# Sign words on GpSimd, a table of shifts for the jobs of two layers, and dummy transposes at the start

## The chip, the cores and the metric

The kernel runs on one core of a Trainium2 chip. The metric is device time in microseconds (us) from start to end of one execution of the whole program. A run of three executions gives a median; beside it stands one further execution that was profiled, and its trace is what this text reads. Engines are called by the names of the profile: PE is the matrix engine (PEld its weight loads), DVE the vector engine, ACT the scalar engine, POOL is GpSimd, SP issues DMAs.

## The reference

Three layers run one after the other on 2304 tokens of width 512 (4 sequences of 576 tokens).

```python
# attention, 8 heads of 64, with rotary positions on q and k
scores = scale * q_rot @ k_rot.T;  attn = softmax(scores);  x = attn @ v
# gated layer, d_ff 1536
gate = 1.0 / (1.0 + np.exp(-(x @ w_gate)))
x = (gate * (x @ w_val)) @ w_out
# third layer, d_ff 1024
h = x @ w_in
solu = h * softmax(h)
y = layernorm(solu) * g_ln @ w_out
```

Activations and results are float32. The five weight matrices arrive as float64.

## The kernel before

**Stages.** Attention runs from 0 to about 290 us over 16 pairs of heads; the gated layer follows to about 716 us and the third layer to the end. Products are made from float32 operands split in a high and a low part (each operand is cast once, and the cast is subtracted from the operand for the low part), so that three matmuls stand for one product; the gated layer and the third layer further use sums of blocks so that seven block products do the work of eight. That leaves much element-wise work for DVE, ACT and POOL: `xst` (sums of blocks of x, L535), `xs` (its cast on ACT, L540, and the subtraction on DVE, L544), `held` (copies of PSUM that a later matmul group needs, L1363), `yst` (copies of finished PSUM banks), `gs` (gate times value).

**Decoding of weights.** A float64 block of 128 x 512 is loaded (`w_load`, an SP DMA) and turned into float32 by integer operations on its two 32-bit words, in `decode`. `w_mag` on ACT (L463) makes the magnitude of the high word; `w_sign` on DVE (L466) takes the sign bit of the high word into the destination; `w_or_mag` (L469) and `w_or_low` (L474), both on DVE, then put magnitude and low word into it. Destinations are the buffers that the trace calls `w` and `rawv`. From `w`, DVE, ACT and POOL make sums (L483) and splits (cast in `w_high`, L486; subtraction in `w_low`, L494, on DVE or POOL). 52 blocks pass through this; 6 of them during attention, in a separate place of the code.

**What sets the order.** Every operation is written down as a job with engine, cost, buffers read and written, and a due time `need`. For the later two layers `run_jobs` (quoted below) places the jobs one by one: PE's jobs stay in the order written; on each other engine, of the jobs ready at the earliest time, the one with the smallest due time goes first; jobs that name two engines go where they can start first. Each engine's instructions then stand in the program in that order, and an engine runs them in that order: an instruction that waits holds up all behind it. POOL also issues the DMAs `yd<-yst` of the gated layer (L1457). Attention has an order of its own, from a table that this change does not touch, so that a job's cost there decides nothing about the order.

**The start.** PE begins with transposes of the first rows of q and k (`tq`, L222, by the matrix `ident`), then the scores `s` (L291), while DVE and ACT copy the transposes out (`st`), reduce (L298) and exponentiate (L303).

## Time and profile before

| | us |
|---|---|
| median of three executions | 914.72 (914.27 to 915.67) |
| the profiled execution | 915.11 |
| its span, first to last instruction | 913.2 |
| PE busy in it | 882.9 (97%) |
| DVE busy | 810.2 (89%) |
| ACT busy | 653.5 (72%) |
| POOL busy | 339.3 (37%) |

The profiled execution took 915.11 us, 0.39 us above the median; 1.9 us of it lie around the span, before the first instruction and after the last one. The shares are means over three stages that differ much, so the text below reads them by stretch.

### The profile page before, as it was taken

Reading aid. Unit: us, or ns where it says so; the run is one execution under the profiler, and the core shown is the slowest. Engines: PE = TensorE matmul, PEld = TensorE weight load, DVE = VectorE, ACT = ScalarE, POOL = GpSimd, SP = SyncE. Lnnn points to the kernel's source line nnn. Section 1 sums busy time; section 2 is a strip of 40 time slices with the busy share of each in tenths; the row PEclk is TensorE's granted clock in tenths of the full one; section 3 lists DMA queues with packets and bytes.
Section 4 is the critical chain, followed back from the end, with each engine's and each line's share of the span. In section 5 each row is a group of like instructions: output and inputs, shape, how many; then the busy total and the mean of one; then the engine's idle time right before and its main releaser. Section 6 shows DMA issues by size and latency. Waiting matters only on the chain.

```text
span 913.2 us, 16106 instructions
## 1 busy us (share of the span) xinstructions
PE 882.9 (97%) x5354; PEld 833.1 (91%) x5354; DVE 810.2 (89%) x1523; ACT 653.5 (72%) x1379; POOL 339.3 (37%) x296
## 2 busy tenths in 40 slices
PE   4999999999999999999999999999999999999998
PEld 3999999999998999999999999999999877888886
DVE  5999999999997798999998999999987499999971
ACT  4999999999995465666667666666565276777751
POOL 7679899898845000011011121212030243233200
PEclk9999999999999999999999999999999999999999
DMA  4667777678663762425275864659599834454332
GB/s 127 159 183 196 205 200 197 184 209 214 155 165 112 221 216 81 151 81 196 86 230 135 260 133 145 129 174 229 179 250 364 185 124 93 99 109 81 81 70 46
DMA packets 120882, 147.33 MB, mean 161 GB/s; under 512 B 44752, under 2 KB 90080, under 8 KB 120800
## 3 DMA queue, kind: packets, MB, share of 16 engines
q1 hardware_dynamic: 113888, 136.87, 51.4%
q0 software_dynamic: 6912, 9.44, 7.1%
q8 instruction: 42, 0.69, 0.3%
q14 instruction: 40, 0.33, 0.1%
HBM read 77.76 MB, written 37.30 MB: 126 GB/s over the span
## 4 chain that ended last, share of the span: by engine, by line
PE 73%; DVE 19%; issue 3%; DMA 2%; ACT 2%; POOL 0%; SPq 0%; DVEq 0%; ACTq 0%
PE s L291 9%; PE av L420 8%; PE te L379 7%; DVE xs L544 2%; PE tq L222 2%; PE far_c L1869 2%; PE far_b L1869 2%; PE far_c L1871 2%; PE far_b L1870 2%; PE far_c L1870 2%; PE far_b L1871 2%; PE tk L400 1%; DVE w L469 1%; PE near_a L630 1%; PE near_a L629 1%
## 5 line engine op out<-in xcount | busy, mean ns | idle before, releaser
L298 DVE TENSOR_REDUCE nm<-s 128x1 f32<-128x576 f32 x144 | 108.2, 752 | 11.5 <-PE s L291 9.0
L303 ACT ACTIVATE e<-s,nm 128x576 f32<-128x576 f32 x144 | 107.7, 748 | 7.4 <-DVE nm L298 6.0
L291 PE MATMUL s<-st 128*128 128x288 f32 x512 | 96.6, 312 | 5.5 <-DVE st L251 3.9
L373 DVE TENSOR_TENSOR et<-te,et 128x512 fp32r<-128x512 f32 x144 | 95.8, 676 | 1.4 <-ACT et L370 1.3
L420 PE MATMUL av<-et,vs 128*128 128x288 f32 x512 | 94.4, 312 | 0.4 <-POOL vs L202 0.4
L1457 POOL DMA_DIRECT2D yd<-yst x40 | 36.0, 1280 | 141.1 <-ACT yst L486 141.1
L370 ACT CAST et<-te 128x512 fp32r<-128x512 f32 x144 | 81.2, 587 | 7.8 <-PE te L379 6.4
L379 PE MATMUL te<-ident,e 128*128 128x128 f32 x576 | 81.9, 274 | 2.5 <-DVE et L373 2.4
L291 PEld LDWEIGHTS s<-st 128*128 128x128 f32 x512 | 75.1, 193 | 6.8 <-ACT st L249 4.2
L420 PEld LDWEIGHTS av<-et,vs 128*128 128x128 f32 x512 | 73.3, 191 | 0.7 <-POOL vs L202 0.6
L379 PEld LDWEIGHTS te<-ident,e 128*128 128x128 f32 x576 | 67.4, 141 | 5.1 <-DVE et L373 2.5
L540 ACT CAST xs<-xst 128x384 fp32r<-128x384 f32 x110 | 50.7, 518 | 13.7 <-DVE xst L535 11.5
L544 DVE TENSOR_TENSOR xs<-xst,xs 128x384 fp32r<-128x384 f32 x112 | 56.4, 548 | 2.2 <-ACT xs L540 2.0
L1538 POOL TENSOR_TENSOR xs<-xst,xs 128x512 fp32r<-128x512 f32 (+1 forms) x14 | 17.5, 1254 | 72.7 <-ACT xs L1535 72.7
L431 POOL TENSOR_TENSOR x_sb<-uw,um 64x576 f32<-64x576 f32 x30 | 43.2, 1439 | 2.5 <-DMA um<-uw 0.4
L494 POOL TENSOR_TENSOR wv<-w,wv 128x512 fp32r<-128x512 f32 (+1 forms) x3 | 5.2, 1743 | 103.3 <-ACT wv L486 103.3
L170 POOL TENSOR_TENSOR turned_t<-raw_t,other_t 128x576 f32<-128x576 f32 (+1 forms) x30 | 40.5, 1369 | 1.2
L463 ACT ACTIVATE mag<-raw_w 128x512 f32<-128x512 f32 x52 | 34.9, 676 | 7.9 <-DMA raw_w<-in_moe_w_val_dram 3.7
L162 POOL TENSOR_TENSOR other_t<-raw_t,rope_sb 128x1152 f32<-128x1152 f32 x14 | 37.4, 2674 | 5.6 <-DMA raw_t<-in_q_dram 4.5
L162 POOL TENSOR_TENSOR raw_t<-raw_t,rope_sb 128x1152 f32<-128x1152 f32 x14 | 37.3, 2664 | 1.1
L1811 POOL TENSOR_TENSOR st<-st,mhalf 128x1 f32<-128x1 f32 x18 | 15.9, 884 | 54.9 <-DVE st L1810 53.7
L629 PE MATMUL near_a<-xs,wg 128*128 128x384 f32 x96 | 32.3, 337 | 2.1 <-ACT held L1363 2.1
(475 smaller groups left out, 3068.4 us busy)
## 6 DMA issues: line engine op xcount, KB each, us to landing
st<-st SPq DMA_DIRECT2D x45, 288.0 KB, 4.0
xst<-xd SPq DMA_DIRECT2D x32, 384.0 KB, 6.0
raw_w<-in_moe_w_out_dram SPq DMA_DIRECT2D x20, 512.0 KB, 4.5
yd<-yst POOLq DMA_DIRECT2D x40, 192.0 KB, 6.5
st<-st SPq DMA_DIRECT2D x47, 144.0 KB, 2.4
raw_w<-in_moe_w_gate_dram SPq DMA_DIRECT2D x12, 512.0 KB, 4.3
raw_w<-in_moe_w_val_dram SPq DMA_DIRECT2D x12, 512.0 KB, 3.7
cd<-mag SPq DMA_DIRECT2D x22, 256.0 KB, 5.5
```

The costliest lines, as they stand in the source:

```text
L162: eng.tensor_mul(out=(o, x)[step], in0=x, in1=w.to_broadcast([P, n, 2, D // 2]))
L291: nc.tensor.matmul(ps[:, j, :HALF], w, x, start=m == 0, stop=m == len(mm) - 1)
L298: nc.vector.tensor_reduce(out=nm, in_=ps[:, :, :HALF], axis=AX.XY, op=ALU.max, negate=True)
L303: nc.scalar.activation(out=e.rearrange("p (j c) -> p j c", j=2), in_=ps[:, :, :HALF], func=AF.Exp, bias=nm, accum_out=sums[i][:, n:n + 1],)
L370: nc.scalar.copy(out=h_out, in_=ps)
L373: nc.vector.tensor_sub(out=l_out, in0=ps, in1=h_out.bitcast(F32))
L379: nc.tensor.transpose(ps[:, r * P:(r + 1) * P], e[:, r * P:(r + 1) * P], ident)
L420: nc.tensor.matmul(av[:, :HALF], *mm[m], start=m == 0, stop=m == len(mm) - 1)
L431: eng.tensor_add(out=x_sb[hp][rows, b * S:(b + 1) * S], in0=uws.pop((i, h))[rows], in1=uws[i][rows])
L540: nc.scalar.copy(out=t[:, 0], in_=here)
L544: l_eng.tensor_sub(out=t[:, 1], in0=here, in1=t[:, 0].bitcast(F32))
L629: nc.tensor.matmul(out, wh, t[:, 0], start=fresh and j == 0, stop=False, skip_group_check=not fresh)
```

## The change

There are four parts. First, `decode` writes a new job `w_zero` on POOL in place of `w_sign` on DVE: the high word, read as a float, times 0.0, which leaves a zero with the word's sign. The job's due time is the same; its cost in the planner is 0.9 and it is not marked as one that holds the port that DVE and POOL share. This concerns 46 of 52 blocks; the 6 in attention stay on DVE. Second, every job of the later two layers gets a name (`place`, and a running number), and a table `SHIFT` of 945 numbers (mean size 8.2 us) is added to the due times by that name. Two offsets `KEEP_I` are smaller. Third, 54 transposes of `ident` into a PSUM bank that nobody reads: 30 before the first `tq`, 10 after the first three, 5, 5 and 4 behind the scores 1, 2 and 3 of the first pair. Fourth, costs and start times of some attention jobs are edited, and one assignment in `qk_bank` is written shorter; neither moves an instruction.

```diff
+    def w_zero(raw, dst):
+        nc.gpsimd.tensor_scalar(out=dst.bitcast(F32), in0=words(raw)[1].bitcast(F32), scalar1=0.0, scalar2=None, op0=ALU.mult)
...
+        idle_ps = ps_av.tile([P, 512], F32, tag="av", name="idle")
+
+        def keep_clock(n):
+            for _ in range(n):
+                nc.tensor.transpose(idle_ps[:, 0:P], ident, ident)
+
+        keep_clock(30)
         first.extend(qk_bank(0, part)[0][2] for part in range(3))
-        pass
+        keep_clock(10)
...
+    IDLE_AFTER = {1: 5, 2: 5, 3: 4}
...
+        def run():
+            found["s", g] = scores(i, n)
+            if i == 0 and n in IDLE_AFTER:
+                keep_clock(IDLE_AFTER[n])
...
+    plain_job, names_of = job, []
+
+    SHIFT = {
+        "again.0.1": -5.9, "again.0.2": -33.5, "again.0.3": -4.4, "again.0.4": -16.7, "again.0.5": -1.4, "again.0.6": -5.6,
...
+    def job(eng, took, fn, reads=(), writes=(), need=0.0, port=None):
+        key = f"{step[0]}.{step[2]}"
+        step[2] += 1
+        names_of.append(key)
+        plain_job(eng, took, fn, reads, writes, need + SHIFT.get(key, 0.0), port)
...
-        job(V, 0.34, lambda: w_sign(raw, dst), (r,), (dst_at,), need - 5, True)
+        job(G, 0.9, lambda: w_zero(raw, dst), (r,), (dst_at,), need - 5, False)
...
-    KEEP_I = {(2, 0): (0, 36.0), (2, 1): (1, 25.0)}
+    KEEP_I = {(2, 0): (0, 30.0), (2, 1): (1, 20.0)}
```

PE's instructions keep their order; only the dummy transposes come in. Its program began like this before, at the very start:

```order
L222 MATMUL tq_0_221<-ident,turned_t 128x128 x4
L222 MATMUL tq_1_226<-ident,turned_t 128x128 x4
L225 MATMUL tq_2_231<-ident,turned_t 128x128
L291 MATMUL s_0_254<-st_0_137 128x288 x4
L291 MATMUL s_1_264<-st_0_137 128x288 x4
L291 MATMUL s_2_279<-st_0_137 128x288 x4
```

And so it begins now:

```order
L674 MATMUL idle<-ident 128x128 x30
L220 MATMUL tq_0_252<-ident,turned_t 128x128 x4
L220 MATMUL tq_1_257<-ident,turned_t 128x128 x4
L223 MATMUL tq_2_262<-ident,turned_t 128x128
L674 MATMUL idle<-ident 128x128 x10
L289 MATMUL s_0_295<-st_0_137 128x288 x4
L289 MATMUL s_1_305<-st_0_137 128x288 x4
L674 MATMUL idle<-ident 128x128 x5
L289 MATMUL s_2_325<-st_0_137 128x288 x4
L674 MATMUL idle<-ident 128x128 x5
```

The dummies need only `ident`; what they stand ahead of is unchanged (line numbers move because the file is longer).

On ACT, at the eleventh group of `held` copies of the gated layer (the profile has it at 575 to 580 us), these rows stood before:

```order
L540 CAST xs_4248<-xst 128x384 x3
L463 ACTIVATE mag_66<-raw_w_65 128x512
L486 COPY yst<-far_a 128x384
L486 COPY yst<-far_b 128x384
L1363 COPY held_4739<-near_a 128x384
L486 COPY yst<-far_d 128x384
L1363 COPY held_4740<-near_c 128x384
```

Now the same place on ACT reads:

```order
L461 ACTIVATE mag_66<-raw_w_65 128x512
L541 CAST xs_4784<-xst 128x384
L541 CAST xs_4303<-xst 128x384 x2
L541 CAST xs_4571<-xst 128x384
L487 COPY yst<-far_b 128x384
L487 COPY yst<-far_a 128x384
L487 COPY yst<-far_d 128x384
L1561 COPY held_4794<-near_a 128x384
L541 CAST xs_4303<-xst 128x384
L487 COPY yst<-far_c 128x384
```

The magnitude went ahead of the casts, and `held<-near_a` now stands behind three copies of `yst`, not two. On DVE, some 10 us earlier in the gated layer, a stretch with two decodes read like this before:

```order
L483 TENSOR_TENSOR w_67<-w_67 128x256 x3
L466 TENSOR_SCALAR w_67<-raw_w_65 128x512
L494 TENSOR_TENSOR wg_4716<-w_67,wg_4716 128x512
L469 SCALAR_TENSOR_TENSOR w_67<-mag_66,w_67 128x512
L494 TENSOR_TENSOR wg_4716<-w_67,wg_4716 128x768
L466 TENSOR_SCALAR w_67<-raw_w_4717 128x512
L544 TENSOR_TENSOR xs_4068<-xst,xs_4068 128x384
L474 SCALAR_TENSOR_TENSOR w_67<-raw_w_65,w_67 128x512
```

The same stretch on DVE now:

```order
L484 TENSOR_TENSOR w_67<-w_67 128x256 x3
L1584 TENSOR_TENSOR gs_1_4792<-far_a,gs_1_4792 128x384
L495 TENSOR_TENSOR wg_4771<-w_67,wg_4771 128x512
L470 SCALAR_TENSOR_TENSOR w_67<-mag_66,w_67 128x512
L495 TENSOR_TENSOR wg_4771<-w_67,wg_4771 128x768
L475 SCALAR_TENSOR_TENSOR w_67<-raw_w_65,w_67 128x512
L545 TENSOR_TENSOR xs_4123<-xst,xs_4123 128x384
L470 SCALAR_TENSOR_TENSOR w_67<-mag_4773,w_67 128x512
```

The two sign words are gone from DVE; the first one now has to be written by POOL between the last sum (L484), which still reads the old `w`, and the `w_or_mag` two rows on (L470). On POOL such a place, with the DMA issues that stand between, reads now:

```order
L467 TENSOR_SCALAR rawv_91<-raw_w_4772 128x512
L1656 DMA yd_147<-yst 128x384 x4
L467 TENSOR_SCALAR w_67<-raw_w_4772 128x512
L467 TENSOR_SCALAR w_67<-raw_w_65 128x512
L1656 DMA yd_147<-yst 128x384 x4
L467 TENSOR_SCALAR w_67<-raw_w_65 128x512
```

Before, POOL had no decode rows there, and the eight DMA issues of one buffer stood together. On ACT, where the third layer starts (the profile has it at 729 to 744 us), the rows before were:

```order
L486 COPY mag_4718<-far_c 128x512
L486 COPY rawv_90<-far_a 128x512
L1535 CAST xs_4068<-xst 128x256
L1535 CAST xs_4068<-xst 128x2x256
L1800 ACT_TABLE_LOAD
L1800 ACTIVATE scr_8760,st_8699<-yst,st_8699 128x1024
L1800 ACTIVATE scr_8761,st_8717<-yst,st_8717 128x1024
```

Now they are:

```order
L487 COPY mag_4773<-far_c 128x512
L2011 ACT_TABLE_LOAD
L2011 ACTIVATE scr_8787,st_8752<-yst,st_8752 128x1024
L2011 ACTIVATE scr_8788,st_8772<-yst,st_8772 128x1024
L1737 CAST xs_4123<-xst 128x256
L487 COPY rawv_90<-far_a 128x512
L2019 ACTIVATE scr_8787,st_8752<-yst,st_8752 128x1024
```

The copy `rawv<-far_a`, which frees a PSUM bank, moved behind the table load and two exponentials. Further on, the copy `mag<-near_c` moved from behind the third exponential to ahead of it. Over the two layers, eight of POOL's `xst` sums (L1544) and its three `wo` subtractions (L1326) moved to DVE, and two 256-wide `xs` subtractions (L1538) the other way.

## Rows read from the trace of the kernel before

**Rows 1.** The page: the span, and the engines' busy time (share, instructions).

```profile
span 913.2 us, 16106 instructions
PE 882.9 (97%) x5354; PEld 833.1 (91%) x5354; DVE 810.2 (89%) x1523; ACT 653.5 (72%) x1379; POOL 339.3 (37%) x296
```

**Rows 2.** Windows: stretch, length, busy time of five engines, granted clock, DMA share, GB/s.

```profile
34.00:280.00 246.00, 245.26 (x1938) 235.72 (x1937) 234.56 (x406) 232.21 (x556) 206.92 (x162) 1.00 0.71 187
340.00:540.00 200.00, 199.41 (x1149) 198.76 (x1148) 185.60 (x371) 135.56 (x291) 21.08 (x20) 1.00 0.51 152
540.00:580.00 40.00, 37.25 (x211) 36.17 (x210) 39.26 (x76) 24.97 (x54) 7.56 (x9) 1.00 0.47 125
```

**Rows 3.** Waits of PE over the whole span: in total, times, longest.

```profile
PE s L291 <- DVE st L251: 3.9, 1, 3.9
...
PE near_a L629 <- ACT held L1363: 2.1, 2, 2.0
PE far_d L1851 <- DVE xs L1860: 1.5, 1, 1.5
PE near_c L1574 <- ACT mag L486: 1.1, 1, 1.1
```

**Rows 4.** Timeline of the start, POOL and PE: start, us, what, idle before.

```profile
1.00 0.29 POOL masks.py:199 TENSOR_SCALAR_AFFINE_SELECT ident<-ident 128x128 f32<-128x128 f32 x1
...
6.89 1.09 PE L222 MATMUL tq<-ident,turned_t 128*128 128x128 f32 x4 [6.89 <-DVE turned_t L170]
...
9.90 0.44 PE L225 MATMUL tq<-ident,turned_t 128*128 128x128 f32 x1
...
31.11 0.60 PE L222 MATMUL tq<-ident,turned_t 128*128 128x128 f32 x4
```

**Rows 5.** Windows of the same kind: six us of the first scores, and the stretch after 580 us.

```profile
18.40:24.80 6.40, 6.31 (x30) 6.28 (x31) 3.22 (x6) 4.15 (x11) 6.32 (x5) 1.00 0.23 51
...
580.40:583.80 3.40, 3.40 (x12) 3.40 (x12) 3.26 (x7) 1.61 (x4) 1.74 (x2) 0.50 1.10 151
```

**Rows 6.** Timeline at 566 us, DVE: a sign word and what follows.

```profile
565.72 0.43 DVE L466 TENSOR_SCALAR w<-raw_w 128x512 int32<-128x512 int32 x1
...
566.06 0.69 DVE L494 TENSOR_TENSOR wg<-w,wg 128x512 fp32r<-128x512 f32 x1
...
566.66 0.68 DVE L469 SCALAR_TENSOR_TENSOR w<-mag,w 128x512 int32<-128x512 int32 x1
```

**Rows 7.** Timeline at 557 us: POOL and DVE side by side.

```profile
557.03 1.28 POOL L494 TENSOR_TENSOR wg<-w,wg 128x512 fp32r<-128x512 f32 x1 [13.68 <-ACT wg L486]
...
557.14 1.72 DVE L469 SCALAR_TENSOR_TENSOR w<-mag,w 128x512 int32<-128x512 int32 x1
```

**Rows 8.** Groups of POOL by shape: busy us, mean ns, idle before.

```profile
L1457 POOL DMA_DIRECT2D yd<-yst x40 | 36.0, 1280 | 141.1 <-ACT yst L486 141.1
...
L494 POOL TENSOR_TENSOR wg<-w,wg 128x256 fp32r<-128x256 f32 x1 | 0.7, 743 | 31.6 <-ACT wg L486 31.6
```

**Rows 9.** Timeline at 575 to 580 us: DVE, ACT and PE.

```profile
575.87 1.45 ACT L540 CAST xs<-xst 128x384 fp32r<-128x384 f32 x3 [1.54 <-DVE xst L535]
...
578.15 0.48 ACT L486 COPY yst<-far_b 128x384 f32<-128x384 f32 x1
578.52 0.49 ACT L1363 COPY held<-near_a 128x384 f32<-128x384 f32 x1
...
579.06 0.44 PE L629 MATMUL near_a<-xs,wg 128*128 128x384 f32 x1 [1.96 <-ACT held L1363]
```

**Rows 10.** Timeline at 729 to 743 us: ACT and PE.

```profile
729.65 0.59 ACT L486 COPY mag<-far_c 128x512 f32<-128x512 f32 x1 [0.96 <-PE far_c L1576]
...
733.49 0.39 PE L1574 MATMUL far_a<-wv,xs 128*128 128x512 f32 x1
...
734.54 1.28 ACT L1800 ACT_TABLE_LOAD   x1
735.83 1.15 ACT L1800 ACTIVATE scr<-yst,st 128x1024 f32<-128x1024 f32 x1
```

More of the change, by code (lines that the diff above doesn't have):

```diff
@@ L214, in qk_bank @@
         raw = turned[i].rearrange("p i h d -> p i (h d)")
-        if part == 0:
-            stacks[i, 0] = st_t[i % 2][0]
-            stacks[i, 1] = st_t[i % 2][1]
+        stacks[i, 0], stacks[i, 1] = st_t[i % 2]
         st = stacks[i, 0]
@@ L730, in job_scores @@
             reads.append(one(f"qtl{i % 2}", 0, 2))
-        took = (1.06 if order[n] is None else 0.53) * (2.0 if g < 4 else 1.0)
+        took = 1.06 if order[n] is None else 0.53
+        if i == 0 and n in IDLE_AFTER:
+            took += 0.11 * IDLE_AFTER[n]
         writes = [one(f"S{g % 2}")] + ([one(f"sum{i % 4}", 0, NTL)] if n == 0 else [])
-        ajob(nc.tensor, took, lambda: found.__setitem__(("s", g), scores(i, n)), reads, writes)
+        def run():
+            found["s", g] = scores(i, n)
+            if i == 0 and n in IDLE_AFTER:
+                keep_clock(IDLE_AFTER[n])
+        ajob(nc.tensor, took, run, reads, writes)
     def job_softmax(g):
@@ L773, in job_attend @@
             e = (A, V)[SLOTS["uw"][2 * h + j]]
-            ajob(e, 0.365 if e is V else 0.3, lambda: high(e, *found["av"][0][1:]), (one("AV"),), (one(uw, *c),))
+            ajob(e, 0.365 if e is V else 0.39, lambda: high(e, *found["av"][0][1:]), (one("AV"),), (one(uw, *c),))
     def job_join(i, h):
@@ L796, in job_weigh_out @@
     def job_weigh_out(i):
-        ajob(V, 0.2, lambda: weigh_out(i, 0), (found.pop(("tr", i)),), (one("rt"),))
+        ajob(V, 0.27, lambda: weigh_out(i, 0), (found.pop(("tr", i)),), (one("rt"),))
         ajob(SP, 0.2, lambda: weigh_out(i, 1), (one("rt"),), (one(f"d{i % 2}"),))
@@ L959 @@
     begin("turned", None)
-    for m, t in enumerate((7.9, 10.0, 10.25)):
+    for m, t in enumerate((7.5, 9.7, 9.85)):
         gate[len(jobs)] = t
@@ L1179, with place @@
     jobs, seen, gate = [], {}, {}
+    plain_job, names_of = job, []
+    SHIFT = {
[156 rows of a table added]
+    }
+    def place(*name):
+        step[:] = [".".join(map(str, name)), None, 0]
+    def job(eng, took, fn, reads=(), writes=(), need=0.0, port=None):
[3 more added lines that the diff above has]
+        plain_job(eng, took, fn, reads, writes, need + SHIFT.get(key, 0.0), port)
     def xs_at(name, j):
@@ L1230, in make_pair @@
     def make_pair(s, n, need):
+        place("pair", s, n)
         for j in range(2):
@@ L1238, in make_plain @@
     def make_plain(n, need):
+        place("plain", n)
         of, done = 1024 * (n % 2), (2, 2, 2, 0)[n]
@@ L1250, in make_again @@
     def make_again(n, need):
+        place("again", n)
         job(SP, 1.7, lambda: nc.sync.dma_start(out=w32[:, 0:1024], in_=wd[n]), (one(f"wd{n}"),), (one("w32", 0, 1024),), need - 12)
@@ L1265, in keep_p @@
     def keep_p(n, need):
+        place("keep", n)
         k = raws_used[0] % 2
@@ L1278, in keep_i @@
     def keep_i(c, need):
+        place("keep_i", c)
         quarter = {f"B{m + 1}{n + 1}": slice(1024 * m + 512 * n, 1024 * m + 512 * n + 512) for m in range(2) for n in range(2)}
@@ L1304, in load_unit @@
     def load_unit(c, need):
+        place("cd", c)
         at_ = C_AT[c]
@@ L1315 @@
     KEEP = {(1, 1): range(0, 5), (1, 2): range(5, 8)}
-    KEEP_I = {(2, 0): (0, 36.0), (2, 1): (1, 25.0)}
+    KEEP_I = {(2, 0): (0, 30.0), (2, 1): (1, 20.0)}
     def make_unit(kind, n, where, need):
+        place("w", kind, n)
         k = raws_used[0] % 2
@@ L1328, in load_x @@
     def load_x(b, need):
+        place("x", *now, b)
         for kk in range(KD):
@@ L1352, in unit @@
     def unit(s, b, n_unit, done=0):
+        place("unit", s, b, n_unit)
         q, kind, setn = n_unit // 2, "gv"[n_unit % 2], n_unit % 2
@@ L1425, in output @@
     def output(s, b, half, setn):
+        place("out", s, b, half)
         bank, need = banks[setn], out_at(s, b, half)
@@ L1463 @@
     END = unit_at(*LAST, 4) + 2 * OUT
+    now = [0]
     for s in range(NF // FG):
+        now[:] = [s]
         if s:
@@ L1525, in job_y @@
     def job_y(p_, need):
+        place("y", p_)
         st = lambda lo, n=1: one("xst", 1024 * (p_ % 2) + 256 * lo, 1024 * (p_ % 2) + 256 * (lo + n))
@@ L1581, in job_h @@
     def job_h(p_, need):
+        place("h", p_)
         names = set_names(p_)
@@ L1633, in job_n @@
     def job_n(t, need):
+        place("n", t)
         ph_at, scr = [e_at(t)], one(f"scr{t % 2}")
@@ L1650, in job_p @@
     def job_p(t, need):
+        place("p", t)
         pk, tp = pk_at(t), one(f"tp{t % NTP}")
@@ L1657, in job_u @@
     def job_u(t, need):
+        place("u", t)
         tp = one(f"tp{t % NTP}")
@@ L1669, in job_turn_ln @@
         hi_w, lo_w = LT_AT[t % 2]
+        had = list(step)
+        place("turn", t)
         for n in range(2):
@@ L1675, in job_turn_ln @@
             job(V, 0.6, lambda n=n: turned_ln(t, n, 1), (at_, hi), (lo,), need + n + 1, False)
+        step[:] = had
     def job_j(t, need):
+        place("j", t)
         at_ = one("bank", 5 + t % 2, 6 + t % 2)
@@ L1703 @@
             names += [f"sg{q_}{x}" for q_ in range(2) for x in "abcd"] + ["held1", "held5", "heldu", "held4"]
+            place("open")
             job(V, 0.01, lambda: open_pools(), (), [one(n, 0, 2) for n in names] + [one("xs4", 0, 4 * HT), one("X")], END + 2, False)
```

12 lines of the change are left out of this document (7 added, 5 removed), and 155 rows, old and new, of the table SHIFT.

## The prediction

> **What bounds the kernel now.** I read the page first, then the time cut into windows, then PE's waits, then the timeline at the few places where PE waits long. The page shows PE busy for 882.9 of 913.2 us [rows 1], so about 30 us could be won at most by keeping PE fed, and a good part of these lie before its first matmul and behind its last. The windows show where PE is the limit already: 245.26 of 246.00 us in the body of attention, and 199.41 of 200.00 us from 340 to 540 [rows 2]. Nothing can be won there by moving work between DVE and POOL, however busy DVE is. What is left is the start, one crowded place at 540 to 580 us, where PE has 37.25 of 40.00 us and DVE 39.26 [rows 2], and the start of the third layer, where PE waits 1.5 us for DVE and 1.1 for ACT [rows 3]. The profiled execution took 915.11 us; I make the sum against that and take off 0.39 us at the end to stand at the median.
>
> **The start.** `ident` is ready at 1.29 us and the first `tq` waits until 6.89 [rows 4]. There four transposes take 1.09 us and one alone takes 0.44; the same four take 0.60 us at 31 us. This is PE at 1.2 GHz and at 2.4 GHz, by the durations: the column of the granted clock shows 1.00 from the first microsecond on, so I don't trust it there. One dummy therefore costs (1.09 - 0.44) / 3 = 0.217 us at the low clock and half of that, 0.11, at the high one. Thirty of them end at 1.29 + 30 x 0.217 = 7.8 us if the clock stays low, 0.9 us after the first `tq` could start, and earlier if it rises on the way. Before the clock rose in the kernel before, PE had been busy for 6.31 of the 6.40 us up to 24.8 [rows 5]; the dummies give PE unbroken work ahead of `tq`, and I take it that the clock rises during them. Then the second group of `tq` is 0.5 us shorter, the first scores are about as much earlier, and of the stretch up to 24.8 us what PE loses by its low clock comes back as far as ACT lets it: ACT works 4.15 of the 6.40 us, so at most 2.25. I take 0.5 + 0.4 + 1.0 = **-1.9 us**. From below -3.2 (0.5 + 0.45 + all of 2.25). From above +3.9, if the clock stays low or falls again before the scores: 0.9 for the first thirty and 14 x 0.217 = 3.0 for those between scores. The ten behind the first three `tq` lie in PE's wait of 3.9 us for the first scores [rows 3], which covers 10 x 0.217 = 2.2 us; without that cover they would cost this much.
>
> **Sign words.** One on DVE lasts 0.43 us, but the next instruction starts 0.34 us after it [rows 6]; DVE's relief is 46 x 0.34 = 15.6 us, all in the gated layer. The price is the time for which POOL stops DVE. A POOL subtraction of 1.28 us stretched a `w_or_mag` on DVE to 1.72 us [rows 7], where it takes 0.68 [rows 6]: 1.04 us lost to one POOL instruction. The trace has no POOL operation with one input at 128 x 512. It lies between nothing and the two-input 128 x 512 at 1.28 us [rows 7]; the nearest row in words read is the two-input 128 x 256, which reads the same 512 values a partition in 0.743 us [rows 8], and I take that. Not every sign word meets such a DVE operation, and one that comes while DVE holds the port waits itself. With DVE losing 1.04 / 1.28 = 0.8 of the POOL time when they meet, and about every second one meeting, 46 x 0.743 x 0.8 x 0.5 = 14 us are given back. The three `wo` subtractions that come back from POOL add 0.6 us each to DVE (start to start, 566.06 to 566.66 [rows 6]) and take away a stretch of up to 1.04 each: 3.1 - 1.8 = 1.3 more. The net relief is 15.6 - 14 + 1.3, about 3 us over the whole layer (bounds: 17 with no meeting, and 46 x (0.34 - 1.04) + 1.3 = -31 with every sign word costing what rows 7 show).
>
> The Trainium skill has the rule behind this: the page "SBUF — State Buffer", section "SBUF: two separate sides", says that the port pair that VectorE and GpSimd share is an exclusive lock, held for the whole instruction, against a VectorE operation with two SBUF inputs. It speaks against the change, and the trace agrees (1.72 us against 0.68). The page "Perfetto Trace Analysis", section "Optimizing Scalar/DVE Operations", draws the conclusion that moving work between these two engines might not help.
>
> **What that does for PE.** PE's only long wait in the gated layer proper is one for a copy `held`, 2.0 of 2.1 us [rows 3]. ACT waits 1.54 us for DVE's `xst`, casts, decodes a magnitude, copies two banks, and only then makes `held`; PE starts 1.96 us late [rows 9]. Behind it the clock is at 0.50 for 3.40 us [rows 5], that is, 1.2 GHz after a PE that had stood still for 2 us; it costs half of 3.40, 1.7 us. DVE has no break ahead of that place (39.26 of 40.00 us), so its backlog is what ACT waits for, and of the net relief I count some 2.2 us ahead of there. That is a little more than 1.96 us, so the wait goes and the fall of the clock with it: -2.0 - 1.7 = -3.7. Against this stand new waits by the new order: `held` stands behind one more copy, 0.37 us (the start to start of [rows 9]), and sign words stand behind four DMA issues of 1.28 us each [rows 8], which wait for copies of `yst` themselves. DVE's `w_or_mag` waits for the sign word and everything behind it on DVE waits too. I take +1.0 for these, between nothing and 5.1 (four issues in a row once). Sum for the gated layer: **-2.7 us**.
>
> **The third layer's start.** `mag<-near_c` goes ahead of the third exponential, so 1.1 us go; the normalising of the first tile starts earlier on DVE, so the 1.5 us go [rows 3]: together -2.6. In turn `rawv<-far_a`, which PE needs at 733.49, stands behind the table load and two exponentials. From the copy before it, 729.65 + 0.59, it is 1.28 + 2 x 1.15 us to the end of the second exponential, 733.8, and a small cast and the copy itself (0.59, like the one at 729.65) come on top [rows 10]: 734.8 at the latest, 1.3 us late. Copies on ACT start 0.37 us apart while each lasts 0.48 [rows 9], so part of that overlaps, and I take +0.8: **-1.8 us**. Bounds: -2.6, and +1.3 if only the new wait comes.
>
> **The sum.** -1.9 - 2.7 - 1.8 = -6.4; 915.11 - 6.4 - 0.39 = **908.3 us** at the median.
>
> **Rivals.**
> - *The port eats the relief.* If POOL takes back all of the 15.6 us (0.34 us per word, a third of what rows 7 show for one), the wait at 579 stays as it is and the gated layer gives nothing: -1.9 - 1.8 = -3.7, 911.0. For it: the price is near that. Against: the order puts less DVE work ahead of the crowded place even so. Chance 0.17.
> - *Slower: sign words hold DVE up for long.* DVE loses b us per word. Its idle time from 340 to 540 us is 14.4 us [rows 2], and the rest of the layer has little. It decides where 46 x (b - 0.34) exceeds 14.4 + 3.7, the gain of the other two parts, at b = 0.73. At b = 0.9 PE would end 46 x 0.56 - 18 = 8 us later, 922.4. For it: 1.04 us in rows 7. Against: that was a POOL instruction of 1.28 us. Chance 0.08.
> - *The dummies don't do what they are for.* The clock stays low at the first scores and PE's extra work costs there: +1.5 in place of -1.9, 911.7. Chance 0.12.
> - *A sign word behind DMA issues.* POOL waits for a `yst` copy, the sign word comes late, and DVE waits in front of `w_or_mag` with PE's copies behind it: three such places at 1.3 us each, +3.9, 912.2. For it: DMA issues now stand between sign words. Against: DVE has 0.7 us of idle at the crowded place only. Chance 0.10.
> - My forecast: 0.53.
>
> The likeliest case has its own range of 905 to 911. With the other cases the range for 8 in 10 is 904 to 913: the upper end takes in all cases but the slower one, the lower one is the full sum of the start (1.3 more), no new wait in the gated layer (1.0), and no late `rawv` in the third (0.8), with something over for waits below half a us that no row here shows. What can be told from no change is about 0.2%, 1.8 us: faster means below 912.9, slower above 916.5. From the cases: faster 0.81 (nearly all of the forecast and most of three rivals), same 0.10, slower 0.09.
>
> **What the changed profile would show.** At the start: four `tq` transposes in 0.60 us, and scores at full speed from the first on. In the gated layer: 46 rows of `w_zero` near 0.74 us, and DVE rows with two inputs that are stretched beside them; no wait of 2 us for `held`, no stretch at clock 0.50 behind 575 us. In the third layer: a wait of about 1 us for `rawv<-far_a`, none of 1.1 for `mag`. The prediction is wrong if `w_zero` takes well above 1 us, if DVE's busy time after 300 us rises, or if a new wait of PE of over 2 us appears before 700 us.

## The result

The changed kernel takes 920.96 us in the median of four runs (919.54 to 921.88), the kernel before 914.50 on the same chip: a ratio of 1.0067, interval 1.0049 to 1.0085. It is slower by some 6 us where 908.3 was forecast. The profiled execution took 921.88 us with a span of 920.1.

The page of the changed kernel, its span and the engines' busy time, beside [rows 1]:

```profile
span 920.1 us, 16248 instructions
PE 894.8 (97%) x5408; PEld 842.3 (92%) x5408; DVE 799.0 (87%) x1482; ACT 656.2 (71%) x1383; POOL 413.2 (45%) x333
```

DVE did become freer, by 11.2 us of busy time, and POOL took 73.9 us more. PE's busy time grew by 11.9 us, since it holds the 54 dummies (10.7 us of PE time in the timeline of the start) and stretches at the low clock. Windows of the changed kernel, of the same kind as [rows 2]; the first two cut the stretches as there, the third is a new one:

```profile
34.00:280.00 246.00, 245.29 (x1938) 235.50 (x1937) 234.41 (x406) 232.25 (x557) 208.25 (x160) 1.00 0.72 187
...
340.00:540.00 200.00, 198.03 (x1130) 195.14 (x1129) 180.35 (x342) 133.86 (x285) 61.37 (x42) 1.00 0.49 146
...
287.00:292.00 5.00, 5.00 (x23) 4.86 (x23) 2.53 (x6) 2.17 (x5) 1.26 (x2) 0.66 0.90 297
```

In the profile of before the stretch behind 287 us is at the full clock:

```profile
287.40:292.00 4.60, 4.54 (x29) 4.36 (x30) 2.74 (x7) 2.40 (x6) 1.27 (x2) 1.00 0.83 274
```

The 200 us that PE filled before now have gaps, 198.03 us busy. Waits of PE over the whole span of the changed kernel, beside [rows 3]:

```profile
PE near_a L630 <- ACT held L1561: 2.5, 2, 1.9
PE s L289 <- DVE st L249: 2.5, 1, 2.5
PE far_b L646 <- DVE wv L495: 2.4, 1, 2.4
...
PE near_a L1636 <- DVE wo L1522: 1.4, 2, 1.1
...
PE far_a L1776 <- ACT rawv L487: 1.1, 1, 1.1
```

The kernel before, from 300 to 340 us, and c_after_plan_dve (the changed order with the sign words on DVE, see the experiments) have the wait for `wv` too:

```profile
PE near_a L1437 <- DVE wo L1326: 0.3, 1, 0.3
PE far_b L645 <- DVE wv L494: 0.3, 1, 0.3
...
PE far_b L646 <- DVE wv L495: 1.8, 1, 1.8
```

The wait for `held` that was to go is still there. Two waits for weights have grown, `wv` from 0.3 to 2.4 us and `wo` from 0.3 to 1.4; with DVE's words in the same order `wv` still costs 1.8, so most of this wait comes with the order and not with POOL. The wait for `rawv` at the third layer's start has come as foretold, and the two for `mag` and `xs` in [rows 3] are gone.

The timeline at 583 to 589 us of the changed kernel, ACT and PE, beside [rows 9]:

```profile
584.52 0.47 ACT L487 COPY yst<-far_b 128x384 f32<-128x384 f32 x1
584.89 0.48 ACT L487 COPY yst<-far_a 128x384 f32<-128x384 f32 x1
585.26 0.49 ACT L487 COPY yst<-far_d 128x384 f32<-128x384 f32 x1
...
585.63 0.50 ACT L1561 COPY held<-near_a 128x384 f32<-128x384 f32 x1
...
586.19 0.44 PE L630 MATMUL near_a<-xs,wg 128*128 128x384 f32 x1 [1.94 <-ACT held L1561]
```

Here the three copies ahead of `held` are seen, 0.37 us apart. PE is as late as before, 1.94 us for 1.96.

The sign words themselves, from the view of the changed kernel's line L467 (durations in ns: least, median, most; then who waited for it, total in us and number of times):

```profile
L467 POOL TENSOR_SCALAR w<-raw_w x26: 1517/1540/2335, 310.0 to 663.5; 128x512 f32<-128x512 f32 x26
L467 POOL TENSOR_SCALAR rawv<-raw_w x20: 1514/1534/7357, 317.4 to 602.4; 128x512 f32<-128x512 f32 x20
...
  DVE w L470: 5.4, 4
  DVE rawv L470: 2.9, 2
```

One takes 1.54 us, not 0.743, and DVE stood still 8.3 us for them. The first of the gated layer shows how, in the timeline at 310 us of the changed kernel, and behind it the same block in the kernel before:

```profile
310.03 1.54 POOL L467 TENSOR_SCALAR w<-raw_w 128x512 f32<-128x512 f32 x1 [18.82 <-DMA raw_w<-in_moe_w_val_dram]
311.60 0.69 DVE L470 SCALAR_TENSOR_TENSOR w<-mag,w 128x512 int32<-128x512 int32 x1 [3.08 <-POOL w L467]
...
308.81 0.43 DVE L466 TENSOR_SCALAR w<-raw_w 128x512 int32<-128x512 int32 x1 [1.52 <-DMA raw_w<-in_moe_w_val_dram]
```

POOL waits for the block to land and needs 1.54 us; the next instruction in DVE's order needs that word, and DVE waits. Before, DVE waited for the landing too, 1.52 us, and then its own 0.43 us stood there; so about 1.5 of the 3.08 us, and of the 8.3 us in all, are the landing. The weights `wv` for which PE then waits 2.4 us come out of such decodes.

PE's instructions stand in the same order in all kernels of this text, so each can be matched with the one of before. This table, worked out from the traces, tells by how many us PE starts the instruction later than before that started in the profile of before at the time in the head; the labels are those of the experiments below.

```
                     36    287    299    336    430    540    600    725    765    905
changed           -0.64  -0.61   0.88   4.13   5.71   7.45   7.41   7.57   6.50   6.54
c_after_plan_dve  -1.52  -1.53  -0.17   1.43   4.93   6.81   4.28   4.68   3.59   3.63
d_before_plan_pool -0.88 -0.67   0.89   4.08   6.10   8.00   7.03   9.89   9.88   9.90
e_beside          -0.59  -0.60  -0.57   1.22   1.34   3.58   4.82   8.16   8.17   8.21
f_short           -0.41   0.80   2.37   2.54   2.82   1.98  -2.28  -2.59  -2.41   1.39
p_no_wait         -0.56  -1.10  -1.10  -0.50  -0.23  -0.03  -2.88  -1.76  -1.58   2.21
s_one_tile         0.00  -0.32  -0.32   0.41   0.69   0.87   0.89   1.32   1.50   5.29
i_act_same_plan   -0.04  -0.53   0.86   2.19   3.88   3.10  -0.19  -0.28  -0.27  -0.23
r_act_from_25     -1.04  -1.51  -1.51  -1.26  -1.26  -1.28  -4.62  -4.25  -4.24  -4.20
```

For the changed kernel: 3.2 us are lost from 299 to 336, another 3.3 up to 540, next to nothing after that, and 1.1 are won in the third layer. The 1.5 us between 287 and 299 are the clock (0.66 in the window above, behind the same wait of 2.2 us for `et` that the kernel before has at 287). That step of 1.4 to 1.6 us is in 11 of the 20 profiles of this study and not in the other 9; of the kernels that keep the order of before, some have it (d_before_plan_pool, f_short, i_act_same_plan) and some do not (e_beside, p_no_wait, r_act_from_25). So a single profile is no better than 1.5 us there; the medians below are over 4 to 12 runs, but for k_pool_prices, which has one.

### The profile page after: what moved, and what is told of

Read it like the earlier page. It is cut to its first block, busy times and chain, and to the rows that moved or that the text cites. A ratio compares the mean times of both kernels' runs of the same rounds, so it can differ in the third digit from the quotient of the medians.

```text
span 920.1 us, 16248 instructions
## 1 busy us (share of the span) xinstructions
PE 894.8 (97%) x5408; PEld 842.3 (92%) x5408; DVE 799.0 (87%) x1482; ACT 656.2 (71%) x1383; POOL 413.2 (45%) x333
## 4 chain that ended last, share of the span: by engine, by line
PE 79%; DVE 13%; ACT 2%; issue 2%; DMA 2%; POOL 1%; SPq 0%; ACTq 0%; DVEq 0%; POOLq 0%
PE s L289 9%; PE av L418 8%; PE te L377 7%; DVE xs L545 2%; PE far_a L630 2%; PE far_a L632 2%; PE far_a L631 2%; PE tq L220 2%; PE far_c L2081 2%; PE far_c L2080 2%; PE far_b L2081 2%; PE far_b L2080 2%; PE far_c L2082 2%; PE far_b L2082 2%; PE tk L398 1%
## 5 line engine op out<-in xcount | busy, mean ns | idle before, releaser
L467 POOL TENSOR_SCALAR w<-raw_w 128x512 f32<-128x512 f32 x26 | 43.3, 1670 | 123.6 <-DVE w L484 35.5
L467 POOL TENSOR_SCALAR rawv<-raw_w 128x512 f32<-128x512 f32 x20 | 39.9, 2048 | 69.4 <-DMA raw_w<-in_moe_w_out_dram 43.7
L545 DVE TENSOR_TENSOR xs<-xst,xs 128x384 fp32r<-128x384 f32 x112 | 61.8, 590 | 0.7 <-ACT xs L541 0.4
L1740 POOL TENSOR_TENSOR xs<-xst,xs 128x512 fp32r<-128x512 f32 (+1 forms) x16 | 20.0, 1260 | 66.7 <-ACT xs L1737 42.8
```

Of the source, the lines that this page charges most:

```text
L467: nc.gpsimd.tensor_scalar(out=dst.bitcast(F32), in0=words(raw)[1].bitcast(F32), scalar1=0.0, scalar2=None, op0=ALU.mult)
L545: l_eng.tensor_sub(out=t[:, 1], in0=here, in1=t[:, 0].bitcast(F32))
```

## The experiments

Ratios are those of the runs of a kernel to runs of the kernel before on the same chip, with their interval.

**Which part makes it slow?** Four kernels. The first puts the sign words of the changed kernel back on DVE and lets the planner plan anew.

```diff
-        job(G, 0.9, lambda: w_zero(raw, dst), (r,), (dst_at,), need - 5, False)
+        job(V, 0.34, lambda: w_sign(raw, dst), (r,), (dst_at,), need - 5, True)
```

> The changed kernel with the 46 sign words back on DVE, planned anew; shifts and dummies stay. Latency theory (a sign word on POOL takes 1.5 us where DVE takes 0.43, and the weights that PE waits for at 300 to 335 us come that much later): the waits of 2.4 and 1.1 us there shrink to below 1 us, time 912.5 to 914.5. Order theory (the table of shifts makes the waits): 919 to 921.

Measured: 934.94 us, 1.0219 (1.0199 to 1.0240). Both expectations missed. The table of shifts does not fit this plan: with one job's engine changed, PE gets new waits of up to 4.9 us.

The second puts the sign words of the kernel before on POOL, with the opposite edit and nothing else.

> The kernel before with nothing but the sign words on POOL, planned anew. Latency theory: waits of PE at 300 to 335 us grow by some 3 us as in the changed kernel, time 918 to 921. Order theory: 914 to 915.5. Port theory (POOL stops DVE): DVE's two-input operations from 300 to 720 us gain over 10 us of busy time and PE waits throughout 340 to 700 us, time above 918.

Measured: 930.04 us, 1.0162 (1.0144 to 1.0179), beyond what the latency and the order theory gave. Sign words on POOL cost 15 us when the planner is left alone with them. Against this, table and dummies of the changed kernel (1.0067) win 8.7 us.

Planning anew changes the order everywhere, so the other two keep the plan and exchange only the engine that executes the word.

```diff
 # c: in the changed kernel, w_zero's body
-        nc.gpsimd.tensor_scalar(out=dst.bitcast(F32), in0=words(raw)[1].bitcast(F32), scalar1=0.0, scalar2=None, op0=ALU.mult)
+        nc.vector.tensor_scalar(out=dst, in0=words(raw)[1], scalar1=-2**31, scalar2=None, op0=ALU.bitwise_and)
 # d: in the kernel before
-        job(V, 0.34, lambda: w_sign(raw, dst), (r,), (dst_at,), need - 5, True)
+        job(V, 0.34, lambda: w_zero(raw, dst), (r,), (dst_at,), need - 5, True)
```

> The changed kernel with its plan unchanged, only that DVE executes the sign words at the places in the plan. Latency theory: the waits at 300 to 335 us go, 914 to 917. Order theory: 919 to 922, since the order is the same. Port theory: the stretch of DVE operations by some 10 us goes, and DVE gains 16 us of sign words, so 914 to 921 does not tell it apart; the mean of the xs subtraction falls from 590 to 548 ns.

Measured: 919.15 us, 1.0042 (1.0028 to 1.0057). The engine makes only some 2 us in this plan (the two intervals overlap); the order theory's range holds it and the latency theory's does not. The other 4 us are there with the words on DVE.

> The kernel before with its plan unchanged, only that POOL executes the sign words. Latency theory: 918 to 922, with the waits at 300 to 335 us. Order theory: 914 to 915.5. Port theory: above 918, with waits of PE spread over 340 to 700 us.

Measured: 923.63 us, 1.0098 (1.0078 to 1.0118). In the plan of before the engine alone makes 9 us, above the latency theory's range and, being spread over the layer, as the port theory had it. So the engine costs 9 us in a plan that was not made for it; the changed plan avoids most of that, but is itself 4 us slower than the old one with the words on DVE. Waits of DVE in d_before_plan_pool from 300 to 725 us show where it stands still (total, times, longest):

```profile
DVE w L472 <- POOL w L469: 11.0, 8, 3.3
...
DVE rawv L472 <- POOL rawv L469: 5.1, 4, 1.6
```

That is 16.1 us (1.9 of them the landing of blocks), as much as the relief that was counted, 15.6.

**Port or lateness?** In the plan of before, three kernels take the two apart. e_beside leaves DVE's words and has POOL make each once more into a spare place, so it has the port and no relief. f_short has the relief and a word of POOL that is short, 64 of 512 columns. p_no_wait has the relief and POOL's words at full length, but nobody waits for them. In f_short and p_no_wait the signs of the weights are left out.

```diff
 # e_beside: job(V, 0.34, ...) calls
+    def w_beside(raw, dst):
+        w_sign(raw, dst)
+        nc.gpsimd.tensor_scalar(out=spare, in0=words(raw)[1].bitcast(F32), scalar1=0.0, scalar2=None, op0=ALU.mult)
 # f_short: the word, and w_or_mag with a zero in place of dst as second operand
+        nc.gpsimd.tensor_scalar(out=dst[:, :64].bitcast(F32), in0=words(raw)[1][:, :64].bitcast(F32), scalar1=0.0, scalar2=None, op0=ALU.mult)
...
+            out=dst, in0=mag.bitcast(I32), scalar=3, in1=none.to_broadcast([P, 512]), op0=ALU.logical_shift_left, op1=ALU.bitwise_or
 # p_no_wait: as f_short, but the word is
+        nc.gpsimd.tensor_scalar(out=spare, in0=words(raw)[1].bitcast(F32), scalar1=0.0, scalar2=None, op0=ALU.mult)
```

> The kernel before, with DVE's sign words as they were; POOL makes each of the 46 once more, into a spare place that nobody reads. So POOL holds the port as in the changed kernel, but nobody waits for its result. Port theory (POOL's time on the shared port stops DVE, and that is the price): DVE's two-input operations gain 10 us or more, 918 to 924. Latency theory (the price is that the word comes late): 913.5 to 916.

Measured: 924.95 us, 1.0103 (1.0090 to 1.0116), just above the port theory's range and far from the other. POOL's 46 words cost 9.4 us though nothing in the trace waits for them. The page of e_beside has DVE busy 10.9 us longer than before with the same 1523 instructions. Groups of DVE in e_beside, 300 to 725 us, show what is stretched, and behind them the same groups before (busy us, mean ns):

```profile
PE 883.3 (96%) x5354; PEld 830.5 (90%) x5354; DVE 821.1 (89%) x1523; ACT 653.2 (71%) x1379; POOL 415.4 (45%) x342
...
L473 DVE SCALAR_TENSOR_TENSOR rawv<-mag,rawv 128x512 int32<-128x512 int32 x20 | 15.5, 777 | 0.6
...
L466 DVE TENSOR_SCALAR w<-raw_w 128x512 int32<-128x512 int32 x27 | 13.8, 515 | 5.0 <-DMA raw_w<-in_moe_w_gate_dram 2.9 <-DMA raw_w<-in_moe_w_val_dram 1.7
...
L469 DVE SCALAR_TENSOR_TENSOR rawv<-mag,rawv 128x512 int32<-128x512 int32 x20 | 14.7, 734 | 0.8 <-ACT mag L463 0.3
...
L466 DVE TENSOR_SCALAR w<-raw_w 128x512 int32<-128x512 int32 x27 | 12.2, 454 | 4.3 <-DMA raw_w<-in_moe_w_gate_dram 2.5 <-DMA raw_w<-in_moe_w_val_dram 1.5
```

> The kernel before with its plan unchanged; POOL makes the sign word of 64 of the 512 columns only, and w_or_mag takes no sign in (signs of the weights are left out). DVE is rid of its sign words, the wait for POOL stays, but is short. If the length of POOL's instruction is the price (latency or port): 912 to 915. If the wait for another engine as such or POOL's place in its queue is the price: 919 to 924. If DVE's relief were worth what was forecast: below 912.

Measured: 914.08 us, 0.9986 (0.9977 to 0.9995): it is the length of POOL's instruction that costs, not the step to another engine as such.

> The kernel before with its plan unchanged; POOL makes the 46 words in full length into a spare place, DVE makes none, and w_or_mag takes no sign in (signs of the weights are left out). So DVE has the relief and POOL holds the port, but nobody waits for POOL. If the port alone is the price and relief and port add up as the runs apart show (-5.0 and +8.7 in the gated layer): 917 to 920. If the late word is most of the price of POOL's plan: 911 to 915. If it makes no difference: 922 to 925.

Measured: 918.78 us, 1.0044 (1.0029 to 1.0059). As it stands this lies in the range of the port alone; the next run changes that reading.

Both kernels lose about 4 us in the third layer (the table, 765 to 905), where PE has no break. They share one new tile of one word a partition, `none`, allocated ahead of most others. A run of the kernel before with that tile alone tells what it does:

```diff
+    none = const.tile([P, 1], I32, name="none")
+    nc.vector.memset(none, 0)
```

> The kernel before with one more constant tile of one word a partition, set to zero once and never read. If the place of the buffers that come after it makes the matmuls of the third layer slower: they start 0.232 us apart in place of 0.227, and the time is 918 to 919.5. If the lost signs did it: 914.5 to 916, as before.

Measured: 921.04 us, 1.0056 (1.0035 to 1.0076), more than expected; the steps from 725 on are those of f_short. So the two times are read against this one. f_short stands at 0.9986 / 1.0056 = 0.993, p_no_wait at 1.0044 / 1.0056 = 0.9988. In us of 914.5: the relief is worth -6.4, the port costs 5.3 on top of it (9.4 where DVE has no relief), and from p_no_wait to d_before_plan_pool the wait for the late word costs 10.1. These are differences of neighbours, so that they sum to the +9.0 of d_before_plan_pool by themselves and the sum is no test of them. The four times come from different sets of runs, each with its own interval, so each term is good to some 2 us. That lateness costs more than the port beside the relief is just clear of that; against the 9.4 of e_beside it is not.

**What does POOL's instruction cost by itself?** The kernel before with eight multiplications on POOL in the last stretch of the third layer, alternately from every second word (`two`) and from words in a row (`there`).

```diff
...
+        for src in (two, there[:, :512], two[:, :256], there[:, :256]):
+            nc.gpsimd.tensor_scalar(out=w32[:, :src.shape[-1]], in0=src, scalar1=0.0, scalar2=None, op0=ALU.mult)
```

> The kernel before, with POOL multiplications by 0.0 in the last stretch of the third layer, where POOL and DVE have little to do: 512 and 256 words a partition, from every second word and from words in a row. If reading every second word makes the 1.5 us: 512 words in a row take 0.5 to 0.8 us. If the form of the instruction does: 1.3 to 1.5 us in a row too, and 256 words 0.7 to 0.8.

Measured at a time when DVE has little to do (busy 1.29 of 7.60 us); groups of POOL in k_pool_prices, 889.4 to 897 us:

```profile
L1914 POOL TENSOR_SCALAR w<-w 128x256 f32<-128x256 f32 x4 | 3.4, 856 | 0.3
L1914 POOL TENSOR_SCALAR w<-w 128x512 f32<-128x512 f32 x2 | 3.0, 1507 | 0.2
```

The two of 512 stand one for each kind and take 1.52 and 1.49 us. The stride is without effect; the form makes the price. It is higher than that of the subtraction of two operands of the same size, 1.28 us [rows 7]. The 256 words took 0.86 us, a little more than expected. The first of 512, at 885 us, where DVE was still busy (3.10 of 4.50 us), took 2.40 us, so POOL too seems to be held up beside DVE.

**The dummies, and the third layer's shifts.** The first kernel is before with the 54 dummies (the diff above), the second has in addition only those shifts whose names belong to the third layer, and the words on DVE.

> The kernel before with the 54 dummy transposes alone. By the traces the start ends 0.6 us earlier: 913.4 to 914.2. If the dummies are worth what was forecast: 912 to 913. If they do nothing: 914.2 to 914.7.

Measured: 915.43 us, 0.9995 (0.9985 to 1.0006): nothing that the runs can tell, and neither the 1.9 us that were forecast nor the loss of 1.5 us of the rival. (The -0.64 us at 36 in the table is no sign of a gain: d_before_plan_pool and e_beside, without dummies, have -0.88 and -0.59 there.) The timeline of PE at the start of the changed kernel, beside [rows 4], shows why:

```profile
1.35 6.29 PE L674 MATMUL idle<-ident 128*128 128x128 f32 x30 [1.35 <-POOL ident masks.py:199]
7.48 0.60 PE L220 MATMUL tq<-ident,turned_t 128*128 128x128 f32 x4
...
13.83 0.46 PE L289 MATMUL s<-st 128*128 128x288 f32 x1 [2.50 <-DVE st L249]
15.27 2.05 PE L289 MATMUL s<-st 128*128 128x288 f32 x7 [0.99 <-ACT st L254]
17.12 1.27 PE L674 MATMUL idle<-ident 128*128 128x128 f32 x5
```

The clock did rise, the first `tq` take 0.60 us in place of 1.09. But PE stands still 2.5 us ahead of the first scores, and behind that seven matmuls of the scores take 2.05 us and five dummies 1.27, 0.21 each: the low clock again (five dummies take 1.27 us at that place in g_dummies_only too).

> The kernel before with the dummies and with the shifts of the third layer's jobs alone; sign words on DVE, the gated layer's order as before. By the changed kernel's trace the start of the third layer gives 1.1 us: 912 to 913.5. If the table only pays in the plan that it was made for: 914 or more.

Measured: 920.35 us, 1.0051 (1.0039 to 1.0063). The shifts of the third layer make a wait of PE of 3.8 us for `mag` there when the rest of the table is missing, so they pay only beside it.

**Is the relief worth anything without the port?** ACT has room from 300 to 720 us (266 of 420 us busy before). These kernels let ACT execute the word in the plan of before, in a new plan, and in the changed plan. The factor 0.0 loses the sign on ACT, so these kernels leave the signs of the weights out.

```diff
 # i: body of the word in the kernel before; l: in the changed kernel; j: also as a job of ACT, cost 0.57
+        nc.scalar.activation(out=dst.bitcast(F32), in_=words(raw)[1].bitcast(F32), func=AF.Copy, scale=0.0)
```

> The kernel before with its plan unchanged; ACT executes the 46 sign words (the high word times 0.0, some 0.67 us each like the magnitude). DVE is rid of them and nothing more holds the port. If the port is what made POOL's words dear and DVE's relief is worth some 5 us, as the run with 64 columns shows in the gated layer: 909 to 912, without the wait of 2 us at 579. If ACT's queue takes its place as the bound: 913 to 918, with longer waits for copies held. If any move of the word off DVE costs by the wait between engines: above 918.

Measured: 913.22 us, 0.9972 (0.9962 to 0.9982). Faster, but by less than expected: by the table it loses 3.0 us from 299 to 430, where the word stands with the magnitude on one engine (that this makes the loss is not shown), and wins 4.1 from there to 600. DVE waits for ACT's words as well, in the view of the word's line L469:

```profile
who waited for it (us, times):
  DVE w L472: 6.6, 9
  DVE rawv L472: 5.8, 10
```

That is 12.4 us, not far below the 16.1 for POOL's, in a kernel that is 2.6 us faster than before and not 9 slower; the waits alone are not the price.

> As the run before, but planned anew with the word as a job of ACT at 0.57. By the port theory 909 to 913; planning anew cost 6 us with the word on POOL (930.0 against 923.6), so up to 918 if the planner's order is the larger share.

Measured: 920.48 us, 1.0047 (1.0031 to 1.0063). The new plan costs 7 us more than the old one with the same words; planning anew cost 6 us with the words on POOL too (b_zero_only against d_before_plan_pool).

> The changed kernel with its plan unchanged; ACT executes the sign words at POOL's places in the plan. Port theory: the 16 us of DVE's relief come without the port, below 919.2 (the same plan with DVE) and below 921.0, at 912 to 916. If the order of the table holds the time: 918 to 921.

Measured: 913.32 us, 0.9973 (0.9962 to 0.9984). In the changed plan, POOL's words cost 8.6 us against ACT's.

Two more make the word on ACT from the magnitude by 2 to the power of -38, in the plan of before and in the changed one. This keeps most signs and loses some.

```diff
+        nc.scalar.activation(out=dst.bitcast(F32), in_=mag, func=AF.Copy, scale=2.0 ** -38)
```

> The kernel before with its plan unchanged; ACT makes the sign words from the magnitude by a factor of 2 to the power of -38, which leaves at most the last bit beside the sign. As the earlier run on ACT (ratio 0.9972) if the lost signs had no part in its time: 911 to 914. If the signs made it fast: 914 to 917.

> The changed kernel with its plan unchanged, its sign words made by ACT in the same way. As the earlier run on ACT in that plan (0.9973): 911 to 914. If the wait between magnitude and sign word on one engine costs: 914 to 918.

Measured: 914.80 us, 0.9997 (0.9988 to 1.0007), and 914.82 us, 0.9991 (0.9980 to 1.0002). Nothing is left of the gain in either. The word now needs the magnitude first, and DVE waits 16.3 us for ACT's words in m_act_signed. That the missing signs made the two faster kernels fast was the other possibility; the next two keep the signs and are faster all the same.

**Only where it wins.** In the plan of before, the first 14 (24) of the 46 words stay on DVE, the others go to ACT with a factor of 2 to the power of -36, which keeps the signs.

```diff
...
+            if at_ == "s":
+                signs[0] += 1
+                if signs[0] <= 14:
+                    return w_sign(raw, dst)
```

> The kernel before with its plan unchanged; the first 14 of the 46 words (to 422 us) stay on DVE, ACT makes the other 32 from the magnitude, with a factor of 2 to the power of -36 that leaves a few of the last bits beside the sign. By the stages of the runs on ACT: nothing lost to 430 us, 0.7 won to 500, 3.3 at 540 to 600: ratio 0.994 to 0.997. If the relief needs the earlier words too (DVE's backlog builds up from the start): 0.997 to 1.000.

Measured: 912.46 us, 0.9970 (0.9960 to 0.9980).

> The same with ACT from the 25th word on (500 us). If the wait at 579 goes by what is taken off DVE in the 80 us ahead of it: ratio 0.995 to 0.998. If the backlog builds up earlier: the wait stays above 1 us, ratio 0.999 to 1.001.

Measured: 911.97 us, 0.9967 (0.9954 to 0.9980). Both are faster than the kernel before, by 3 us, and than the changed one. Moving 22 words is as good as moving 32. The timeline of ACT at 575 us in r_act_from_25:

```profile
572.27 1.45 ACT L543 CAST xs<-xst 128x384 fp32r<-128x384 f32 x3 [1.54 <-DVE xst L538]
...
574.92 0.49 ACT L1380 COPY held<-near_a 128x384 f32<-128x384 f32 x1
```

The `held` copy of [rows 9] comes 3.60 us earlier, while PE itself is 2.8 us earlier there by waits that are gone ahead of it (0.53 us at 547, 0.26 at 564), what follows them, and the 1.3 us that it was ahead at 540; the wait is 1.12 us in place of 1.96, and the stretch at the low clock behind it is gone (1.00 from 576.4 to 580).

**DVE's account.** The pages give one more reading of all these runs: how much DVE's busy time changed, how long it waited for the words, and what the time did (in us of 914.5; the last two kernels against c_after_plan_dve, which has their order, f_short and p_no_wait against s_one_tile).

| | busy | waits | sum | time |
|---|---|---|---|---|
| e_beside | +10.9 | 0 | +10.9 | +9.4 |
| d_before_plan_pool | -8.4 | 16.1 | +7.7 | +9.0 |
| m_act_signed | -14.8 | 16.3 | +1.5 | -0.3 |
| i_act_same_plan | -14.7 | 12.4 | -2.3 | -2.6 |
| q_act_from_15 | -12.1 | 8.0 | -4.1 | -2.7 |
| r_act_from_25 | -9.6 | 5.5 | -4.1 | -3.0 |
| f_short | -12.1 | 1.4 | -10.7 | -6.4 |
| p_no_wait | -7.7 | 0 | -7.7 | -1.1 |
| changed | -7.5 | 8.3 | +0.8 | +2.3 |
| l_after_plan_act | -14.4 | 5.1 | -9.3 | -6.3 |

The time goes with the sum to some 2 us in seven of the ten; f_short, l_after_plan_act and above all p_no_wait win less than their sum. So it is a reading and no law, but it fits POOL losing where ACT wins: in the plan of before, the words on ACT free 14.7 us of DVE and on POOL 8.4, and the waits are longer.

## Why the prediction was wrong

By the table, the stages of the changed kernel give -0.6 us to 36, +1.5 at 287 (the clock), +3.2 from 299 to 336, +3.3 to 540, 0.0 to 600, +0.2 to 725 and -1.1 in the third layer. The forecast had -1.9, -2.7 and -1.8. It is the gated layer that failed, with the new waits that were put at +1.0 and the wait for `held` that was to go.

**What bounds the kernel** was read rightly in part. Places at which DVE's backlog makes PE wait exist, and relief there is worth something: -6.4 us with a short word of POOL, -3 us with ACT's. What was not seen is that a stretch in which PE is full has something to lose. Of 340 to 540 us the prediction says "Nothing can be won there", and it sets no term for it; PE lost 3.3 us from 336 to 540. At 299 to 336 it lost 3.2, at its waits for fresh weights and by the low clock behind them (0.60 from 317.8 to 322 us). With DVE's words in the same order this stretch still loses 1.6.

**The price of a sign word** is the first step that failed: "the nearest row in words read is the two-input 128 x 256, which reads the same 512 values a partition in 0.743 us [rows 8], and I take that". It is 1.54 us, outside the bounds that were drawn from the rows (nothing to 1.28). The price goes by the elements of the instruction, 1.51 us for 512 and 0.86 for 256, and one operand is not cheaper than two.

**The meetings on the port** were over-counted for a word of that length. By the forecast POOL gives back 14 of the 15.6 us of relief; with 1.54 us the same product gives 28. By DVE's busy time, in the plan of before, the words on ACT free 14.7 us and on POOL 8.4, so 6.3 are given back; in the changed plan 14.4 and 7.5, so 6.9. The net relief in busy time was thus larger than the 3 us of the forecast, and it is not here that the sign turned. The stretch itself is real: e_beside pays 9.4 us for it. This is where the rule of the Trainium skill, page "SBUF — State Buffer", section "SBUF: two separate sides", stood; the trace agrees as far as a mean over all words tells (734 to 777 ns for `w_or_mag` into `rawv`, which has two inputs).

**The waits by the new order** are the step on which the sign turned: "I take +1.0 for these, between nothing and 5.1". The mechanism was named, DVE waiting at `w_or_mag` with everything behind it, but put down to DMA issues ahead of the word on POOL. At the places of the changed kernel where DVE waits, POOL waits for the block to land or for DVE's last reader of the old word, and then takes 1.5 to 1.9 us; no DMA issue stands there. (In d_before_plan_pool some stand ahead of the words, at 488 and 534 us.) DVE waits 8.3 us in the changed kernel, which is more than the 7.5 us it was freed of, and 16.1 in the plan of before. Order and engine do not simply add up: in the order of before the words give 0 on DVE, -2.6 on ACT and +9.0 on POOL, in the new order +3.8, -2.5 and +6.1 us. So against DVE in the same order POOL costs only some 2 us of the 6, and the other 4 are there with the words on DVE; against ACT, which brings the relief without the port, POOL costs 8.6 and turns a gain into a loss. For the new order the forecast had only the 0.37 us of one more copy ahead of `held` and the places of the sign words; what in it costs 4 us while DVE has its words is open.

**The rival of slower** came nearest to the time, 922.4 by DVE losing 0.9 us a word, and had a chance of 0.08. Its mechanism is not what the trace shows: stretch and waits together are 6.9 + 8.3 us for 46 words, 0.33 us each. That its time is near is luck.

**The wait at 579** was to go with the clock behind it, -3.7. It is there with 1.94 us, and from 540 to 600 nothing is won. With words on ACT in the plan of before it shrinks to 1.2 us and less, and these 60 us win 3.3 (i_act_same_plan, r_act_from_25); with DVE's words in the changed order they win 2.5. So the size was right for a DVE that does not wait for POOL.

**The start**, -1.9: the runs show no gain, by the reason given for the upper bound (the clock falls again before the scores), but also not the loss that went with it.

**The third layer's start**, -1.8: the trace gives 7.57 to 6.50, -1.1. The new wait for `rawv` is 1.11 us (forecast 0.8), and the waits of 1.1 and 1.5 us are gone but for 0.3 us. This term was right in kind and nearly in size.

**The clock at 287** was not in the sum; with the order of before it can go either way too, as the 20 profiles show.

Two of the three signs of being wrong came: `w_zero` takes well above 1 us, and PE has a new wait of 2.4 us before 700 us. DVE's busy time after 300 us did not rise.

Left open: why the changed plan with words on DVE loses 3.5 us from 336 to 430, and what part of the table does that. No run takes the table apart; a_sign_dve and h_late_shift show only that parts of it do not pay outside their plan.

## What to carry to other kernels

An engine that is busy 89% of the time is not a bound by that alone; moving its work away pays only where another engine waits for it last. When a link in a chain from a landing DMA to the waiting engine is moved, count what the old engine is freed of against what it then waits for the new one: here 14.7 against 12.4 us on ACT, 8.4 against 16.1 on POOL. Exchange the engine alone in a fixed plan first, then plan anew: here a new plan alone changed the time by 6 to 16 us, as much as the effect or more. Price an operation that no row shows by its own form, by a trial at an idle place, before building on it.

## What the runs showed of the hardware

A POOL multiplication by a constant over 128 x 512 float32 takes 1.49 to 1.54 us, strided or not, more than a subtraction of two operands of that size (1.28). Beside a busy DVE one took 2.40 us, and DVE's operations with two inputs are stretched beside it (734 to 777 ns on the mean of 20).

One more constant tile of one word a partition, ahead of the other tiles, makes the matmuls of the third layer take 395 ns in place of 389, at a granted clock of 1.00, and the kernel 5 us longer, of which the profile has 3.8 from 765 to 905 us. Groups of PE in s_one_tile, 800 to 860 us:

```profile
L1576 PE MATMUL near_a<-wg,xs 128*128 128x512 f32 x15 | 5.9, 396 | 0.0
...
L1871 PE MATMUL far_c<-wo,xs 128*128 128x512 f32 x12 | 4.7, 395 | 0.0
```

In the kernel before the matmuls of these lines have 389 ns. That the place of the operands in memory does it is the likely reason, but no run here separates it.

A multiplication by 0.0 on ACT (Copy with a factor) does not leave the sign on the zero, on POOL it does: the result of i_act_same_plan has the same relative error, 9.93, as that of f_short, which takes no signs in.
